# One weight load moved ahead of an activation tile, a filler product left out, two small loads moved back

## The chip, the cores and the metric

The kernel runs on one core of a Trainium2 chip. The core has a matrix engine (TensorE, PE in the profile), three engines for element work (VectorE or DVE, ScalarE or ACT, GpSimd or POOL), a queue engine that here only issues transfers (SyncE, SP) and 16 DMA engines. The metric is the device time of one execution in microseconds, as the median of several runs.

## The reference

The input x has 2048 tokens of 512 values. It is normalised over its 512 values (mean and variance, eps 1e-5). Two things are computed from the result xn and combined:

```python
Lam_bar = exp(dt * Lam);  B_bar = ((Lam_bar - 1) / Lam)[:, None] * Bmat
h = Lam_bar * h + (xn @ B_bar.T)[t]              # 2048 steps, 512 complex states
s = 2 * (h @ Cmat.T).real + xn * Dskip
g = silu((gelu(xn @ w_gate) * (xn @ w_up)) @ w_down)   # 512 -> 1376 -> 512
out = x + s * g
```

Inputs and output are bf16.

## The kernel before, in words

**Tiling.** The tokens are cut into four slabs of 512, each slab into four tiles of 128 tokens (m = 0 to 3). Slab 0 is the start of the program and is treated in a way of its own. The weights w_gate (`wg`), w_up (`wu`) and w_down (`wd`) are loaded once and stay. A product needs x with the channels on the partitions, so tiles are turned: the first three tiles of slab 0 by TensorE itself (`head_t`, with an identity matrix, into PSUM, and copied by DVE or ACT into `xcT`), everything else by DMA transposes on SP's queue (`dma_t4` for a normalised slab into `xnT`, `at_t` for a tile of the gated hidden values `at` into `atT`, and one each for the B and C matrices).

**The head.** `dummies` gives TensorE seven products of constants. `center(m)` takes the mean from a tile of x: ACT sums (L342, L350), DVE subtracts (L346, L351). `head_t(m)` turns it (L316, L331). `parameters` turns the small vectors (L606, L607). `fill` is one more product of constants into a bank that is free at that time (L305). `up_rows(m, k)` is a pair of products of row block k of w_up (128 rows, columns 0 to 1023) with tile m, into two PSUM banks (L391); the four row blocks are four loads. `first_w` does the other columns and w_gate (L421), ACT evacuates (L401, L428), `first_at` multiplies the halves (L434, L436). While that runs, DVE and GpSimd prepare statistics, angles and tables of the scan. `skip` multiplies normalised tiles by the row of D (`Drow`, L372).

**Later.** `half` makes the inputs of the scan (L550), rotates, scans and rotates back on DVE (L562 to L581) into the states `hst`; `down_pair` is the product with w_down (L484), `y_tile` the product of the states with C (L500) and the output; `gate_tile` the gated products of slabs 1 to 3 (L452).

**The order of the work.** Each step is added to a plan with the names that it reads and writes. `Plan.run` emits the steps in the order of the tuple `ORDER`, which was written out by a planner beforehand; costs and due times in the calls are the planner's and have no effect here. Each engine runs its own instructions strictly in that order, and waits on semaphores where it needs another engine's or a transfer's result. All large loads, DMA transposes and stores stand in SP's queue, in this order at the start: x tiles 0, 1, 2; w_up's four row blocks; the rest of w_up; x tile 3; w_gate in two parts; w_down's last 96 rows (L686); slab 1 of x (L217); D's row, spread over the partitions (L687); the turn of slab 0 (L367); the two turns of B (L237); the turn of `at` tile 0 (L468); w_down's other 1280 rows (L685); the turns of `at` tiles 1 and 2; the turn of slab 1; the load of slab 2; and so on. Transfers report on eight semaphores that are used in turn; a transfer is issued only when the one that used its semaphore before has landed.

Of the kernel before, what the change touches and what calls it, by code (L numbers as in the profile page):

```python
# [18 lines left out]


ORDER = (
# [23 lines left out]
)  # L45


# [33 lines left out]
def kernel(  # L81
# [46 lines left out]
    def sb(name, shape, dt=BF16):  # L128
        return consts.tile(shape, dt, name=name)
# [4 lines left out]
    wu = sb("wu", [P, KT, F])  # L134
# [50 lines left out]
    def pe(n, cols, emit, reads=(), writes=(), **kw):  # L185
        return pl.add(PE, n * (cols + 6) / 2400.0, emit, reads, writes, lag=0.22, **kw)
# [17 lines left out]
    def dma_sp(end, landed, emit, writes, **kw):  # L204

        n = dma(SP, end - sp_at[0], landed - end, emit, writes=writes, after=list(sp_last), not_before=sp_at[0], svc=(1, 0.0, 0.0), **kw)
        sp_at[0] = end
        sp_last[:] = [n]

    def load_w(nm, k0, k1, c0, c1, end, landed):  # L210

        w, r = w_of[nm]
        dma_sp(end, landed, lambda: nc.sync.dma_start(out=w[:, k0:k1, c0:c1], in_=r[:, k0:k1, c0:c1]),
               [(nm, k, c) for k in range(k0, k1) for c in range(3) if c0 <= CH[c][0] < c1])
# [6 lines left out]
    def load_x(m, end, landed):  # L221
        dma_sp(end, landed, lambda: nc.sync.dma_start(out=x_tok[:, m, :], in_=x_r[:, m, :]), [("x", 0, m)])

    W2 = CH[1][1]
    load_x(0, 1.12, 2.92)
    load_x(1, 1.59, 3.35)
    load_x(2, 2.06, 3.75)
    load_w("wu", 0, 1, 0, W2, 2.53, 5.1)
    load_w("wu", 1, 2, 0, W2, 3.0, 6.3)
    load_w("wu", 2, 3, 0, W2, 3.5, 7.4)  # L230
    load_w("wu", 3, 4, 0, W2, 4.0, 7.9)
# [53 lines left out]
    def rstd(m0, m1):  # L285

        def f():
            if m0 in BN:
                G.tensor_scalar(out=ve[:, m0:m1], in0=mv[:, m0, 1:2], scalar1=EPS, scalar2=None, op0=ALU.add)
            else:  # L290
                G.tensor_scalar(out=ve[:, m0:m1], in0=ss[:, m0:m1], scalar1=1.0 / D, scalar2=EPS, op0=ALU.mult, op1=ALU.add)
            G.tensor_tensor(out=rs[:, 0, m0:m1], in0=ve[:, m0:m1], in1=mhalf[:, m0:m1], op=ALU.pow)
        return pool(0.65 + 0.2 * (m1 - m0), f, [("mv", m) if m in BN else ("ss", m) for m in range(m0, m1)] + ["mhalf"], [("rs", 0, m) for m in range(m0, m1)],
             rank=250.0 - 20 * m0)
# [7 lines left out]
    def fill(k, i):  # L302
        def f():
            for _ in range(k):
                T.matmul(ring[i][:], lhsT=warm[:, 0:P], rhs=warm, start=True, stop=True)  # L305
        pe(k, 512, f, [], [("bank", i)])

    def head_t(m):

        if m == 0:  # L310
            for i in range(2):
                tp = ring[2 + i][:].bitcast(BF16)[:, 0 : D // 2].rearrange("p (k t) -> p k t", t=P)

                def f(i=i, tp=tp):
                    for k in range(2):
                        T.transpose(tp[:, k, :], xn[0][:, (2 * i + k) * P : (2 * i + k + 1) * P], ident[:])  # L316
                pe(2, P, f, [("xc", 0, i), "ident"], [("bank", 2 + i)])
            for i in range(2):
                tp = ring[2 + i][:].bitcast(BF16)[:, 0 : D // 2].rearrange("p (k t) -> p k t", t=P)
                dst = xcT[:, 2 * i : 2 * i + 2, 0:P]  # L320
                if i == 0:
                    head.append(dve(256, lambda tp=tp, dst=dst: V.tensor_copy(out=dst, in_=tp), [("bank", 2)], [("xcT", 0, 0)], rate=2.0, rank=500.0, after=head[-1:]))
                else:
                    acts(256, lambda tp=tp, dst=dst: act(out=dst, in_=tp, func=AF.Copy), [("bank", 3)], [("xcT", 0, 1)], rank=500.0)
            return
        bank, key = ybank[(m + 1) % 2], ("y", (m + 1) % 2)
        tp = bank[:].bitcast(BF16)[:, 0:D].rearrange("p (k t) -> p k t", t=P)

        def f():
            for k in range(KT):  # L330
                T.transpose(tp[:, k, :], xn[m][:, k * P : (k + 1) * P], ident[:])  # L331
        pe(KT, P, f, [("xc", m, 0), ("xc", m, 1), "ident"], [key])
        dve(512, lambda: V.tensor_copy(out=xcT[:, :, m * P : (m + 1) * P], in_=tp), [key], [("xcT", m, 0), ("xcT", m, 1)], rate=2.0, rank=310.0 - 20 * m)
# [331 lines left out]
        rstd(m, m + 1)  # L665
    stats(M - 1)
    rstd(M - 1, M)
    fill(1, 0)
    head_t(1)
    up_rows(0, 0)  # L670
    up_rows(1, 0)
# [174 lines left out]
```

## Time and profile before

| | us |
|---|---|
| median of 3 runs | 178.81 (178.15 to 179.05) |
| the profiled execution, device time | 178.7 |
| its span in the profile | 176.9 |
| TensorE busy | 172.0 (97% of the span) |
| VectorE busy | 157.0 (89%) |
| ScalarE busy | 123.8 (70%) |
| DMA, mean over the span | 105 GB/s |

The page of the profile lists the busy time of each engine, the span in 40 slices, the chain of work that ended last, and the costliest groups of instructions. A group is named by line, engine, operation and tiles: "L391 PE MATMUL ring<-wu,W" is a product of line 391 that reads `wu` and writes a PSUM bank of `ring` (`xcT` is a view of the tile `W`, so it shows under that name). Times in the views are microseconds from the start of the span. A matrix product's length in a row includes its way through the array; what counts in a row of many is the distance of their starts. A transfer's "us to landing" runs from the start of its issue on SP's queue to the last of the 16 counts that its DMA engines add to its semaphore.

### The profile page before, as it was taken

To read this page: it belongs to the slowest core of one execution; us is meant where nothing else is said; L and a number is where in the kernel's file an instruction comes from. 1 tells how busy PE (TensorE), PEld (TensorE's weight loads), DVE (VectorE), ACT (ScalarE), POOL (GpSimd) and SP (SyncE) were. 2 spreads that over 40 slices of the span, in tenths; PEclk is the share of its full clock that TensorE was granted. 3 is DMA by queue.
4 is the path that set the end of the run, shared out by engine and by line. 5 is a ranking of instruction groups with operands and counts; after the bars stand their busy time and mean duration, and the time that the engine had idled before them with its cause. 6 is when DMAs were issued, how large, how long until landed. Compare 5 with 4: busy or idle time off the path is not lost.

```text
span 176.9 us, 2403 instructions
## 1 busy us (share of the span) xinstructions
PE 172.0 (97%) x830; PEld 82.6 (47%) x846; DVE 157.0 (89%) x252; ACT 123.8 (70%) x236; POOL 11.3 (6%) x25
## 2 busy tenths in 40 slices
PE   8999999999999999999999999999999999999992
PEld 2554554444455544444445454444444455444451
DVE  3759999999798993999979999899999999999764
ACT  6499969969999999799578855373158618582240
POOL 2660030000200000000040000000000000000000
PEclk9999999999999999999999999999999999999999
DMA  5999999997000809423000074094000007718022
GB/s 150 311 372 230 201 235 261 205 284 143 0 0 0 200 1 186 98 79 62 0 0 6 30 139 93 31 191 85 0 0 0 0 30 158 68 34 160 26 76 76
DMA packets 48467, 18.66 MB, mean 105 GB/s; under 512 B 40296, under 2 KB 47944, under 8 KB 48456
## 3 DMA queue, kind: packets, MB, share of 16 engines
q1 hardware_dynamic: 48432, 18.52, 48.7%
q8 instruction: 6, 0.10, 0.3%
q14 instruction: 5, 0.04, 0.1%
q10 hardware_dynamic: 24, 0.00, 0.0%
HBM read 6.46 MB, written 2.10 MB: 48 GB/s over the span
## 4 chain that ended last, share of the span: by engine, by line
PE 94%; DVE 2%; DMA 1%; issue 1%; DVEq 0%
PE ring L452 31%; PE ring L484 21%; PE ring L550 16%; PE ybank L500 15%; PE ring L421 5%; PE ring L391 3%; PE ybank L421 2%; DMA x_tok<-in_A_x_dram 1%; DVE yg L505 1%; DVE junk L511 1%; PE ybank L331 0%; PE ring L316 0%; DVE yg L344 0%; PE ring L305 0%; DVE xna L346 0%
## 5 line engine op out<-in xcount | busy, mean ns | idle before, releaser
L452 PEld LDWEIGHTS <-xnT 128*128 128x128 bf16 x288 | 28.2, 98 | 28.4
L484 PE MATMUL ring<-wd,atT 128*128 128x512 bf16 (+1 forms) x171 | 38.9, 379 | 0.3
L452 PE MATMUL ring<-wg,xnT 128*128 128x512 bf16 (+1 forms) x142 | 31.4, 356 | 0.1
L452 PE MATMUL ring<-wu,xnT 128*128 128x512 bf16 (+1 forms) x142 | 31.2, 356 | 0.1
L550 PE MATMUL ring<-xnT,BT 128*128 128x512 bf16 x128 | 30.1, 379 | 0.0
L581 DVE TENSOR_TENSOR_SCAN Fs<-rho,ini,W 128x512 bf16<-128x512 f32 x24 | 29.7, 1271 | 0.1
L455 ACT ACTIVATE ub<-ring 128x512 bf16<-128x512 f32 (+1 forms) x36 | 19.2, 555 | 14.1 <-PE ring L452 14.0
L500 PE MATMUL ybank<-C,hst 128*128 128x512 bf16 x115 | 27.3, 379 | 0.3
L484 PEld LDWEIGHTS <-atT 128*128 128x128 bf16 (+1 forms) x176 | 17.2, 98 | 20.8
L552 ACT ACTIVATE U<-ring 128x512 bf16<-128x512 f32 x32 | 18.2, 600 | 7.5 <-PE ring L550 7.5
L455 ACT ACTIVATE gt<-ring 128x512 bf16<-128x512 f32 (+1 forms) x36 | 19.5, 555 | 3.7 <-PE ring L452 3.5
L500 PEld LDWEIGHTS <-hst 128*128 128x128 bf16 x136 | 13.3, 98 | 14.0
L550 PEld LDWEIGHTS <-BT 128*128 128x128 bf16 x128 | 12.5, 98 | 14.7
L487 ACT ACTIVATE g<-ring 128x512 f32<-128x512 f32 x16 | 9.4, 595 | 14.2 <-PE ring L484 14.2
L562 DVE TENSOR_TENSOR Q<-U,tab 128x4096 bf16<-128x4096 bf16 x8 | 18.3, 2289 | 0.9 <-ACT tab L649 0.7
L562 DVE TENSOR_TENSOR Q<-Fs,tab 128x4096 bf16<-128x4096 bf16 x8 | 18.3, 2287 | 0.1
L505 DVE TENSOR_TENSOR yg<-ybank,g 128x512 bf16<-128x512 f32 x15 | 10.2, 686 | 5.8 <-PE ybank L500 5.7
L764 ACT ACTIVATE junk<-x_tok 128x512 bf16<-128x512 bf16 x16 | 10.0, 633 | 0.8 <-DMA x_tok<-in_A_x_dram 0.8
L496 ACT ACTIVATE ybank<-sk 128x512 f32<-128x512 bf16 x15 | 9.1, 604 | 1.7 <-DVE yg L505 1.6
L769 ACT ACTIVATE xna<-x_tok,nb,rs 128x512 bf16<-128x512 bf16 x12 | 9.5, 812 | 0.0
L581 DVE TENSOR_TENSOR_SCAN Fs<-rho,W 128x512 bf16<-128x512 f32 x8 | 9.3, 1210 | 0.1
L461 DVE TENSOR_TENSOR at<-gt,ub 128x1024 bf16<-128x1024 bf16 x12 | 8.2, 684 | 0.1
(140 smaller groups left out, 170.6 us busy)
## 6 DMA issues: line engine op xcount, KB each, us to landing
x_tok<-in_A_x_dram SPq DMA_DIRECT2D x3, 512.0 KB, 4.1
out_dram<-ot SPq DMA_DIRECT2D x11, 128.0 KB, 1.8
wd<-in_B_w_down_dram SPq DMA_DIRECT2D x1, 1280.0 KB
wu<-in_B_w_up_dram SPq DMA_DIRECT2D x4, 256.0 KB, 4.1
wg<-in_B_w_gate_dram SPq DMA_DIRECT2D x1, 864.0 KB
x_tok<-in_A_x_dram SPq DMA_DIRECT2D x4, 128.0 KB, 2.1
wg<-in_B_w_gate_dram SPq DMA_DIRECT2D x1, 512.0 KB, 6.3
out_dram<-ot SPq DMA_DIRECT2D x6, 64.0 KB, 1.6
```

The lines of the kernel that those rows point to most:

```text
L421: T.matmul(ps[:, 0 : b - a], lhsT=lhs(k), rhs=wt[:, k, a:b], start=(k == 0), stop=(k == KT - 1))
L452: T.matmul(ps[:, 0 : b - a], lhsT=xnT[:, s % 2, m, k, :], rhs=wt[:, k, a:b], start=(k == 0), stop=(k == KT - 1))
L455: acts(b - a, lambda: act(out=dst[:, a:b], in_=ps[:, 0 : b - a], func=AF.Copy if up else AF.Gelu_apprx_tanh), [("bank", r)], [key], table= ...
L484: T.matmul(ps[:], lhsT=atT[:fs, k, m * P : (m + 1) * P], rhs=wd[:fs, k, :], start=(k == 0), stop=(k == NFT - 1))
L500: T.matmul(ps, lhsT=hst[s % 2][:, j // NPT, j % NPT, m * P : (m + 1) * P], rhs=C2[:, j // NPT, j % NPT, c0:c1], start=(j == 0 and not seed ...
L505: dve(w, lambda: V.tensor_tensor(out=yg[e][:, c0:c1], in0=ps, in1=g2[gi][:, b, c0:c1], op=ALU.mult), [key, ("g2", gi, b)], [("yg", e, c0)])
L550: T.matmul(ps[:], lhsT=BT[:, ri, k, pt * P : (pt + 1) * P], rhs=xnT[:, s % 2, :, k, :], start=(k == 0), stop=(k == KT - 1))
L552: acts(512, lambda q=q, ri=ri, ps=ps: act(out=U[ui][:, ri, q, :], in_=ps[:], func=AF.Copy), [("bank", r)], [("U", ui, q, ri)])
L562: dve(4096, lambda: V.tensor_tensor(out=Qf, in0=src.unsqueeze(1).to_broadcast(WQ), in1=table, op=ALU.mult), reads, ["Q"], rate=2.0)
L581: pl.add(DVE, 1.12 if s == 0 else 1.185, lambda ri=ri, q=q, pt=pt, first=first: V.tensor_tensor_scan(out=Fs[:, ri, q, :], data0=rho[:, pt ...
L764: acts(512, lambda i=i, fn=fn, sc=sc, m=m: act(out=junk()[:], in_=x_tok[:, s * M + m, :], func=fn, scale=sc, accum_out=sx[:, s, i, m : m + ...
L769: acts(512, lambda m=m: act(out=xn[m], in_=x_tok[:, s * M + m, :], func=AF.Identity, scale=rs[:, s, m : m + 1], bias=nb[:, s, m : m + 1]), ...
```

## The change

Four things are different.

- w_up's first row block is loaded ahead of x's tile 2; the two loads change places.
- The filler product is no longer in the program, and `ORDER`, which counts the steps, is one shorter.
- On TensorE the turn of x's tile 1 follows that of tile 0 at once, ahead of the parameters' turns; the turn of tile 2 comes after three pairs of products (block 0 with tiles 0 and 1, block 1 with tile 0) instead of one, and the pairs of tile 2 are shifted accordingly. ACT copies its half of the first turn before it sums tile 2; DVE copies its half before the parameters, and takes tile 0's statistics before it copies tile 2's turn.
- In SP's queue D's row and w_down's last 96 rows no longer stand between w_gate and the turn of slab 0. After the turn of `at` tile 0 the order is now: D's row, w_down's 1280 rows, w_down's last 96 rows, the turn of `at` tile 1. The four products with D's row of slab 0 on DVE follow `at` tile 2 instead of standing between the `at` tiles, and one of the table products (L642) goes ahead of `at` tile 2.

From there on, every engine's order is the one of before.

```diff
 ORDER = (
-    21, 22, 23, 24, 25, 0, 27, 26, 20, 18, 19, 17, 1, 40, 15, 16, 13, 14, 2, 42, 3, 4, 5, 28, 29, 30, 31, 34, 60, 33, 44, 45, 41, 61, 35, 32, 63, 43,
+    21, 22, 23, 24, 25, 0, 27, 26, 20, 18, 19, 17, 1, 40, 15, 16, 13, 14, 2, 3, 4, 5, 28, 29, 30, 31, 33, 42, 44, 45, 41, 60, 34, 32, 62, 61, 63, 67,
...
     load_x(0, 1.12, 2.92)
     load_x(1, 1.59, 3.35)
-    load_x(2, 2.06, 3.75)
-    load_w("wu", 0, 1, 0, W2, 2.53, 5.1)
+    load_w("wu", 0, 1, 0, W2, 2.06, 4.7)
+    load_x(2, 2.53, 5.0)
     load_w("wu", 1, 2, 0, W2, 3.0, 6.3)
...
     stats(M - 1)
     rstd(M - 1, M)
-    fill(1, 0)
+
     head_t(1)
     up_rows(0, 0)
     up_rows(1, 0)
```

44 rows, old and new, of the table ORDER are left out of this document.

## The prediction

> **What bounds the kernel now.** I read the page's busy shares and the chain that ended last first. They say who sets the end:
>
> ```profile
> PE 172.0 (97%) x830; PEld 82.6 (47%) x846; DVE 157.0 (89%) x252; ACT 123.8 (70%) x236; POOL 11.3 (6%) x25
> PE 94%; DVE 2%; DMA 1%; issue 1%; DVEq 0%
> ```
>
> The list of waits of TensorE from 4 us on is empty: once it has x's first tile, it never stands still until the last tile's tail. So the end is TensorE's start, plus its work, plus whatever idle time a change puts in. A gain must be work taken off TensorE; a loss is any wait that it now meets. Next, TensorE in order of time over the first 11 us (start, length, count):
>
> ```profile
> 1.57 2.34 PE L299 MATMUL ring<-const-bfloat16-1.0 128*128 128x512 bf16 x5
> 4.03 0.61 PE L316 MATMUL ring<-ident,xna 128*128 128x128 bf16 x4
> 4.57 0.18 PE L606 MATMUL ybank<-ident,pv 4*128 4x4 bf16 x1
> 4.62 0.16 PE L607 MATMUL ybank<-ident,pv 8*128 8x8 bf16 x1
> 4.71 0.61 PE L305 MATMUL ring<-const-bfloat16-1.0 128*128 128x512 bf16 x1
> 5.12 0.62 PE L331 MATMUL ybank<-ident,xna 128*128 128x128 bf16 x4
> 5.54 0.62 PE L391 MATMUL ring<-wu,W 128*128 128x512 bf16 x2
> 6.00 0.39 PE L331 MATMUL ybank<-ident,xna 128*128 128x128 bf16 x4
> 6.25 4.92 PE L391 MATMUL ring<-wu,W 128*128 128x512 bf16 x22
> ```
>
> Two paces are seen. The five dummies follow each other in (2.34 - 0.63) / 4 = 0.427 us; the 22 products in (4.92 - 0.38) / 21 = 0.216 us. The first pair of products still has 0.25 us between its starts, so the fast pace comes at about 5.6 us. A 128-column turn takes 0.107 us before that and 0.056 after.
>
> Then the DMA issues of w_up's four row blocks, each from a narrow window around its issue (KB, us to landing):
>
> ```profile
> wu<-in_B_w_up_dram SPq DMA_DIRECT2D x1, 256.0 KB, 3.0
> wu<-in_B_w_up_dram SPq DMA_DIRECT2D x1, 256.0 KB, 3.6
> wu<-in_B_w_up_dram SPq DMA_DIRECT2D x1, 256.0 KB, 4.5
> wu<-in_B_w_up_dram SPq DMA_DIRECT2D x1, 256.0 KB, 5.2
> ```
>
> Their issues begin at 2.11, 2.59, about 3.07 and 3.54, so they land at 5.1, 6.2, 7.6 and 8.75 (the counts of their semaphores in the trace say 5.13, 6.17, 7.60 and 8.75).
>
> Last, SP's queue and TensorE where the later transfers go, and the DMA's load there (last two columns: share of the 16 engines, GB/s):
>
> ```profile
> 20.88 1.74 SPq L468 DMA_TRANSPOSE atT<-at  x1
> 22.66 0.63 SPq L685 DMA_DIRECT2D wd<-in_B_w_down_dram  x1
> 23.85 7.11 SPq L468 DMA_TRANSPOSE atT<-at  x2
> 31.29 2.25 SPq L367 DMA_TRANSPOSE xnT<-xna  x1
> ```
> ```profile
> 31.32 2.97 PE L484 MATMUL ring<-wd,atT 128*128 128x512 bf16 x12
> ```
> ```profile
> 24.00:24.50 0.50, 0.50 (x5) 0.35 (x4) 0.50 (x3) 0.49 (x2) 0.00 (x0) 1.00 0.53 152
> 24.50:25.00 0.50, 0.50 (x4) 0.21 (x3) 0.50 (x2) 0.38 (x1) 0.00 (x0) 1.00 1.11 170
> 25.00:25.50 0.50, 0.50 (x5) 0.20 (x3) 0.50 (x3) 0.10 (x2) 0.00 (x0) 1.00 0.70 229
> 25.50:26.00 0.50, 0.50 (x4) 0.26 (x3) 0.50 (x2) 0.50 (x1) 0.00 (x0) 1.00 1.06 315
> ```
>
> By the semaphores w_down lands at 30.18, the second and third turned tiles of `at` at 32.17 and 33.18. The down product takes tile 0, then tile 2 (in the written order), each 11 x 0.216 = 2.38 us: tile 2 is wanted at 31.32 + 2.38 = 33.70. Its cover is only 0.5 us. This is the place to watch.
>
> **The change part by part.** The profiled execution took 178.7 us with a span of 176.9, 0.1 below the median of 178.81; I count against it.
>
> *The filler (L305) goes.* The next start follows it by 5.12 - 4.71 = 0.41 us, at the slow pace. That is the most the head can give.
>
> *The order at the head.* x's first tile is loaded first as before, so its turns stay at 4.03 to 4.43. x's second tile is centred by 4.39, so its four turns follow at once (to 4.86), then the parameters' two with the same 0.14 us around them as now. The first product can start at about 5.15. w_up's first block has one issue (0.47 us) and one tile of x less ahead of it: the second tile landed at 3.25, and the block took 1.1 us after its predecessor, so about 4.4 to 4.7. No wait; but even the old 5.13 would have done.
>
> First product pair 5.15 to 5.79 (its first half at 0.427), second pair to 6.22. The next needs block 1 (6.17): just there; to 6.65. The turn of x's third tile: its load now lands at about 5.1 instead of 4.04, its sum and centring take until 6.3 (rows of 0.63, 0.19 and 0.35 us), so TensorE meets it ready; to 6.90. One more pair to 7.33. The next needs block 2, and that lands at 7.60: TensorE waits 0.3 us. It restarts at 7.63, and after two more pairs, at 8.49, it has done what it now has done at 6.25 + 10 x 0.216 = 8.41. So the head gives nothing: +0.07. The bytes ahead of blocks 1 to 3 are the same as before, which is why they don't move; block 3 is wanted at 9.36 and covered. Bounds: -0.41 (filler fully won, block 2 0.4 us earlier) and +0.3 (block 2's first increment comes 1.6 us before its last, so one slow DMA engine can move it).
>
> *Other engines at the head.* ACT's copy of the first turn goes ahead of the third tile's sum; DVE's statistics (0.68 + 0.18) go ahead of the copy of the third turn, which is then ready at 7.6 and wanted at 8.06. The parameters' copy comes 0.7 us later, GpSimd's power after it too, but DVE takes it up at 7.58 now and 7.65 then. ACT's first evacuation (9.33) slips by 0.1; TensorE wants that bank at 12.2. Cost nothing. w_up's tail now waits for block 0's semaphore (eight are reused in turn), 4.06 to about 4.6; landed 9.75, wanted 11.01: 0.7 us would still be hidden.
>
> *Early SP queue.* w_down's last rows and D's row (issues of 0.91 and 1.10 us, 224 KB) leave. Behind them only the turn of slab 0 and the two of B come sooner; slab 0's is landed at 19.57 and used at 19.77, without a wait, so nothing is gained. The skip products move behind other DVE work of the same sum; D's row has until 25.4.
>
> *Late SP queue.* Between the first turned tile (issue done 22.62) and the second now stand D's row, w_down, w_down's last rows. An issue of such a size took 0.40 us (x's tiles) in the free queue and 1.10 in the full one. Each delays all behind it: the turns of tiles 1 and 2, slab 1's, slab 2's load, C's. Data: 224 KB at 315 GB/s are 0.7 us; the two slots from 24.0 to 25.0 are half empty, but w_down's own start-up fills them and moves by D's issue. I take D's issue at 0.55 (nearest the free queue, since 22.6 follows a single turn) plus 98 KB at 315 GB/s, 0.31: all that follows lands 0.85 us later. Bounds 0.3 and 1.4. Tile 2 then lands at 34.03; TensorE, 0.07 late, wants it at 33.77: a stall of 0.3 us (bounds 0 and 0.8). w_down itself at 30.7 is wanted at 31.4, its last rows at 31.1 at 33.5. Slab 1's turn 35.6 + 0.6 against 38.5, slab 2's load delays ACT by 0.6 at 37.69, where the banks between 47 and 55 us still have 0.7 to 1.0 us. DVE's states are done at 64.27 and wanted at 64.87; both move by about 0.3. No second stall.
>
> Sum: 178.7 + 0.07 + 0.3 = **179.1 us**.
>
> The clock's pace is where a rule speaks against the change. By the rows, the dummies end at 3.9 and until 5.6 TensorE has 0.41 us of filler now, 0.43 of real products then, and the same turns; so I leave the moment of 5.6 as it is. The Trainium skill, "TensorE: Matmul & The Clock Gate", Part 1, says that the clock is released only after a busy window of some 3.4 us, which runs free of the kernel's start, and Part 4 says that turns on TensorE don't count as busy. By that, a head of nothing but turns from 4.03 to 5.15 could miss a window; no row here shows whether turns count. That case is rival D, priced there from rows.
>
> **The rivals.**
> A (forecast): blocks of w_up take the filler's gain, tile 2 stalls a little: 178.8 to 179.6. Against it: the 33.70 is only missed if the delay exceeds 0.5.
> B: the delay of the turned tiles stays under 0.5, as the half-empty slots would allow, and block 2 comes sooner: 178.7 - 0.41 to 178.7 + 0.07, say 178.5.
> C, slower: D's and the last rows' issues take 1.10 and 0.91 us as they did in the early queue. Then tile 2 comes 1.4 us or more later, at 34.6 and after, and the stall is 0.8 to 1.3: 179.6 to 180.1, say 179.9. It decides from a delay of about 1.4 us. For it: the second turn's issue took 4.65 us (23.85 to 28.5), so the queue was full there.
> D, slower: the fast pace comes late. If it needs as long from 4.03 as it took from the first dummy at 0.76 (4.8 us), it comes at 8.85, and 3.3 us at half pace cost 1.6: 180.4.
> E, faster: the denser start brings the fast pace forward to 4.03; 1.55 us at half pace are 0.78, and with the filler 1.2: 177.5.
> F: nothing changes, because the swap buys only what block 0 had anyway; it is inside B.
>
> **How the numbers follow.** Faster or slower by 0.5% (0.9 us) is about what a measurement here can tell from no change. Chances: A 0.48, B 0.22, C 0.17, D 0.07, E 0.06. Faster is E: 0.06. Slower is C above 179.7, D and a tail of A: 0.13 + 0.07 + 0.04 = 0.24. The same: 0.70. The range leaves out E, D and a sliver of both B and C: 178.3 to 180.1.
>
> **What would show it.** No L305; TensorE's first product at 5.15; one wait for a w_up block at about 7.4; a DVE queue unchanged in sum; SP's second `atT` issue at 24.4 or later; a TensorE wait at 33.8 for `atT`. Wrong if the pace changes at another time than 5.6, if block 2 lands well off 7.6, or if tile 2 lands before 33.7.

## The result and the profile after

The changed kernel takes 179.90 us as the median of 6 runs (179.63 to 180.14), the kernel before 178.93 (178.15 to 179.18, 6 runs). The ratio is 1.0066, 95% interval 1.0046 to 1.0086: slower by two thirds of a per cent, beyond the half per cent that can be told from no change. The forecast was 179.1 and no change; 179.9 lies in the range given, but near its upper end and among the cases of the slower sign.

The profiled execution took 180.14 us with a span of 178.4, against 178.7 and 176.9 before. It is the slowest of its six, so the 1.44 us between the two profiles are more than the 0.97 between the medians. Busy times and the chain of the page after (first line: busy us, share of the span, instructions; then the chain's shares by engine and by line):

```profile
PE 172.7 (97%) x845; PEld 82.0 (46%) x845; DVE 156.9 (88%) x252; ACT 123.5 (69%) x236; POOL 12.5 (7%) x25
PE 78%; DMA 10%; DVE 9%; POOL 1%; SPq 1%; issue 0%; DVEq 0%
PE ring L452 31%; PE ring L484 20%; PE ybank L500 15%; PE ring L550 12%; DMA Drow<-in_A_Dskip_dram 3%; DMA x_tok<-in_A_x_dram 3%; DMA atT<-at 3%; DMA wu<-in_B_w_up_dram 2%; DVE Q L642 2%; DVE st L280 2%; DVE sk L372 1%; DVE yg L505 1%; DVE at L434 1%; DVE tab L642 1%; POOL rho L614 1%; DVE junk L511 1%
```

TensorE's busy time has not moved by more than 0.7 us, but its share of the chain fell from 94% to 78%: the chain now leaves TensorE and runs through transfers, and D's row (`Drow`) is one of its links. The list of TensorE's waits, empty before from 4 us on, has four rows between 4 and 45 us (us in total, times, longest); from 45 us to the end it is empty before and after:

```profile
PE ring L391 <- DMA wu<-in_B_w_up_dram: 0.8, 2, 0.6
PE ring L484 <- DMA atT<-at: 0.5, 1, 0.5
PE ring L484 <- DMA wd<-in_B_w_down_dram: 0.2, 1, 0.2
PE ring L316 <- DVE xna L346: 0.2, 1, 0.2
```

The last row is the very first turn, which begins at 4.07 instead of 4.03. The other three are the three places where the time went. (A row counts idle time from the end of the product before. That end includes some 0.16 us of its way through the array, 0.38 - 0.216, so TensorE loses about 0.16 us more at each such wait than the row says.) The head first; TensorE in order of time (start, length, what; in brackets the idle time before it that a release ended):

```profile
4.07 0.40 PE L316 MATMUL ring<-ident,xna 128*128 128x128 bf16 x4 [0.16 <-DVE xna L346]
4.49 0.40 PE L331 MATMUL ybank<-ident,xna 128*128 128x128 bf16 x4
5.21 1.02 PE L391 MATMUL ring<-wu,W 128*128 128x512 bf16 x4 [0.19 <-DMA wu<-in_B_w_up_dram]
6.85 0.59 PE L391 MATMUL ring<-wu,W 128*128 128x512 bf16 x2 [0.61 <-DMA wu<-in_B_w_up_dram]
7.28 0.38 PE L331 MATMUL ybank<-ident,xna 128*128 128x128 bf16 x4
7.50 4.05 PE L391 MATMUL ring<-wu,W 128*128 128x512 bf16 x18
11.39 1.36 PE L421 MATMUL ybank<-wu,W 128*128 128x352 bf16 x8
```

Block 0 landed at 5.17, and the first product waits 0.19 us for it. The four products of block 0 are over at 6.2, and the next pair stands until 6.85, because block 1 landed at 6.81 (6.17 before). The pace was fast from 3.99 on here and from 5.58 before, which, with the filler gone, won a part of that back. L421 begins at 11.39 where it was 11.01 before: the head lost 0.38 us.

Then SP's queue and TensorE around the down product, after:

```profile
20.94 2.28 SPq L468 DMA_TRANSPOSE atT<-at  x1
23.27 0.58 SPq L687 DMA_DIRECT2D Drow<-in_A_Dskip_dram  x1
23.89 0.43 SPq L685 DMA_DIRECT2D wd<-in_B_w_down_dram  x1
24.37 0.66 SPq L686 DMA_DIRECT2D wd<-in_B_w_down_dram  x1
25.12 7.71 SPq L468 DMA_TRANSPOSE atT<-at  x2
```
```profile
32.10 2.54 PE L484 MATMUL ring<-wd,atT 128*128 128x512 bf16 x11 [0.24 <-DMA wd<-in_B_w_down_dram]
35.11 4.93 PE L484 MATMUL ring<-wd,atT 128*128 128x512 bf16 x22 [0.47 <-DMA atT<-at]
```

Before, all three tiles of the down product ran without a break from 31.32. Now it starts at 32.10, 0.40 more than the head's 0.38, and stands again before tile 2, which starts at 35.11 instead of 33.70. So the profile's 1.44 us are 0.38 at the head, 0.40 at w_down, 0.63 at tile 2 and 0.03 in all the rest. By the counts of their semaphores w_down landed at 32.06 (30.18 before) and tile 2 at 35.07 (33.18): 1.9 us later each.

What took so long is seen in the stretches of the DMA's rate (us; busy time and instructions of each engine; the last three columns are TensorE's clock, the share of the 16 DMA engines, GB/s), after:

```profile
24.00:24.50 0.50, 0.50 (x6) 0.30 (x4) 0.49 (x1) 0.50 (x2) 0.50 (x1) 1.00 1.12 248
24.50:25.00 0.50, 0.50 (x5) 0.29 (x3) 0.00 (x0) 0.37 (x2) 0.50 (x1) 1.00 0.30 88
25.00:25.50 0.50, 0.50 (x4) 0.26 (x3) 0.07 (x1) 0.46 (x1) 0.39 (x1) 1.00 0.37 57
25.50:26.00 0.50, 0.50 (x4) 0.23 (x3) 0.50 (x2) 0.14 (x1) 0.00 (x0) 1.00 0.64 139
26.00:26.50 0.50, 0.50 (x4) 0.20 (x2) 0.45 (x2) 0.45 (x1) 0.00 (x0) 1.00 0.72 123
26.50:27.00 0.50, 0.50 (x4) 0.24 (x3) 0.00 (x0) 0.28 (x1) 0.00 (x0) 1.00 0.52 125
27.00:27.50 0.50, 0.50 (x4) 0.25 (x3) 0.00 (x0) 0.32 (x1) 0.00 (x0) 1.00 0.83 197
```

Before, the slots from 25.5 to 27.5 ran at 270 to 332 GB/s, while w_down was in flight; two of them:

```profile
26.00:26.50 0.50, 0.50 (x4) 0.23 (x3) 0.50 (x1) 0.23 (x2) 0.00 (x0) 1.00 0.95 270
26.50:27.00 0.50, 0.50 (x4) 0.20 (x2) 0.50 (x2) 0.50 (x2) 0.00 (x0) 1.00 1.05 332
```

Now, from 24.5 to 27.0, only 57 to 139 GB/s move, while D's row and w_down are both in flight. D's 16 counts come from 25.40 to 28.07, a spread of 2.7 us. VectorE stands for it, and ScalarE behind VectorE (waits of all engines, after):

```profile
DVE sk L372 <- DMA Drow<-in_A_Dskip_dram: 1.6, 1, 1.6
ACT xna L769 <- DVE sk L372: 1.3, 1, 1.3
```

### The profile page after: what moved, and what is told of

Same layout as the page of the kernel before. It is cut to its first block, busy times and chain, and to the rows that moved or that the text cites. A ratio compares the mean times of both kernels' runs of the same rounds, so it can differ in the third digit from the quotient of the medians.

```text
span 178.4 us, 2418 instructions
## 1 busy us (share of the span) xinstructions
PE 172.7 (97%) x845; PEld 82.0 (46%) x845; DVE 156.9 (88%) x252; ACT 123.5 (69%) x236; POOL 12.5 (7%) x25
## 3 DMA queue, kind: packets, MB, share of 16 engines
HBM read 6.46 MB, written 2.10 MB: 48 GB/s over the span
## 4 chain that ended last, share of the span: by engine, by line
PE 78%; DMA 10%; DVE 9%; POOL 1%; SPq 1%; issue 0%; DVEq 0%
PE ring L452 31%; PE ring L484 20%; PE ybank L500 15%; PE ring L550 12%; DMA Drow<-in_A_Dskip_dram 3%; DMA x_tok<-in_A_x_dram 3%; DMA atT<-at 3%; DMA wu<-in_B_w_up_dram 2%; DVE Q L642 2%; DVE st L280 2%; DVE sk L372 1%; DVE yg L505 1%; DVE at L434 1%; DVE tab L642 1%; POOL rho L614 1%; DVE junk L511 1%
## 5 line engine op out<-in xcount | busy, mean ns | idle before, releaser
L484 PE MATMUL ring<-wd,atT 128*128 128x512 bf16 (+1 forms) x176 | 39.5, 379 | 0.7 <-DMA atT<-at 0.5
L552 ACT ACTIVATE U<-ring 128x512 bf16<-128x512 f32 x32 | 18.1, 598 | 7.0 <-PE ring L550 7.0
```

Source lines behind the costliest of these rows:

```text
L484: T.matmul(ps[:], lhsT=atT[:fs, k, m * P : (m + 1) * P], rhs=wd[:fs, k, :], start=(k == 0), stop=(k == NFT - 1))
L552: acts(512, lambda q=q, ri=ri, ps=ps: act(out=U[ui][:, ri, q, :], in_=ps[:], func=AF.Copy), [("bank", r)], [("U", ui, q, ri)])
```

## The experiments

They ran on three chips, each with the kernel before beside it, whose median was 178.77, 178.84 or 178.66 us; each time is a median of 7 to 12 runs. In `ORDER` as changed, 115 is the step of D's row and 114 that of w_down's last rows.

**e1_head_only: the head's part alone.** D's row, w_down's last rows and the skip products stand where they stood before; the rest is the changed kernel.

```diff
-    106, 108, 95, 97, 101, 103, 107, 109, 112, 211, 212, 215, 216, 122, 98, 99, 209, 210, 213, 214, 104, 105, 124, 217, 218, 110, 111, 136, 137, 139,
+    106, 108, 95, 97, 101, 103, 107, 109, 114, 112, 211, 212, 215, 216, 122, 98, 99, 209, 210, 213, 214, 217, 115, 136, 137, 139, 141, 143, 145, 147,
...
```

> The changed kernel with D's row and w_down's last rows loaded early again, and the products with D's row back between the at tiles: the head of the change alone. Theory L (the late loads make the loss: they delay the turned tiles of at, and TensorE stands until tile 2 lands at 35.1 us): that wait is gone, tile 2 lands near 33.2 and is wanted near 34; the time is that of before plus whatever the head costs, 178.9 to 179.3. Theory H (the head makes the loss: with x's third tile behind it, w_up's blocks land late, 0.4 us in the profiled execution, and all follows): 179.5 to 179.9, little below the changed kernel.

Measured: 179.04 us against 178.77, ratio 1.0020 (1.0006 to 1.0034). The head gives nothing and costs about 0.27 us. The profiled execution, at 178.7 the fastest of its twelve, shows only the wait (TensorE in order of time):

```profile
4.91 1.06 PE L391 MATMUL ring<-wu,W 128*128 128x512 bf16 x4
6.49 0.59 PE L391 MATMUL ring<-wu,W 128*128 128x512 bf16 x2 [0.52 <-DMA wu<-in_B_w_up_dram]
11.02 1.36 PE L421 MATMUL ybank<-wu,W 128*128 128x352 bf16 x8
```

Block 1 came at 6.45, and L421 began at 11.02, as before. How the other profiles with this order of loads stand is told with e7.

**e2_late_only: the other half alone.** The head of before, with its filler and its loads; D's row and the last rows late, the skip products moved.

```diff
-    load_w("wu", 0, 1, 0, W2, 2.06, 4.7)
-    load_x(2, 2.53, 5.0)
+    load_x(2, 2.06, 3.75)
+    load_w("wu", 0, 1, 0, W2, 2.53, 5.1)
...
+    fill(1, 0)
```

> The kernel of before with D's row and w_down's last rows moved late and the products with D's row moved as in the change; the head with the filler and the old loads stays. Theory L: the turned tile 2 lands at the same absolute time as in the changed kernel, about 35.1 us, whatever the head did; TensorE, 0.4 us ahead, stands there 1.3 us instead of 0.9, and the whole loss of 1.0 us is there: 179.8 to 180.0. Theory H: about half of it, 179.3 to 179.5, since head and late part add.

Measured: 179.61 us, ratio 1.0045 (1.0024 to 1.0066). With e1's 1.0020 this gives 1.0065, the whole change's 1.0066: two losses that add, the later one the larger. TensorE at the down product:

```profile
31.22 2.54 PE L484 MATMUL ring<-wd,atT 128*128 128x512 bf16 x11
34.24 4.93 PE L484 MATMUL ring<-wd,atT 128*128 128x512 bf16 x22 [0.49 <-ACT U L552]
```

Tile 2 was wanted at 31.22 + 2.38 = 33.60 and began at 34.24, 0.04 after it had landed (34.20); the releaser named there, a row of ScalarE (L552), ended at the same moment but is not the one that matters: in e8 TensorE starts the same product at 35.37, 0.1 us before that row of ScalarE ends. The stall is 0.64, as in the whole change (35.11 - 34.48 = 0.63). Theory L had said that tile 2 lands at 35.1 whatever the head did, and a stall of 1.3; it landed 0.9 us sooner, because the queue ran ahead in this profile: the first turned tile landed at 24.19 instead of 25.09, and D's row was issued at 22.05 instead of 23.27. The counts of D's row are spread as in the whole change, from 24.44 to 27.36.

**e3_d_early and e4_rows_early: which of the two loads.** The whole change, once with D's row (115) and once with w_down's last rows (114) back in the early queue.

```diff
-    106, 108, 95, 97, 101, 103, 107, 109, 112, 211, 212, 215, 216, 122, 98, 99, 209, 210, 213, 214, 104, 105, 124, 217, 218, 110, 111, 136, 137, 139,
-    141, 143, 145, 147, 138, 140, 142, 144, 146, 148, 11, 155, 159, 174, 156, 160, 12, 157, 161, 176, 178, 151, 115, 129, 219, 158, 180, 135, 222,
+    106, 108, 95, 97, 101, 103, 107, 109, 112, 211, 212, 215, 216, 122, 98, 99, 209, 210, 213, 214, 104, 105, 124, 217, 218, 110, 111, 115, 136, 137,
+    139, 141, 143, 145, 147, 138, 140, 142, 144, 146, 148, 11, 155, 159, 174, 156, 160, 12, 157, 161, 176, 178, 151, 129, 219, 158, 180, 135, 222,
```

> The changed kernel with D's row alone loaded early again (w_down's last rows stay late). Theory S (the spread of D's row over 128 partitions is slow by itself, some 2 us for 128 KB, as its packets of 24.5 to 27 us were): w_down lands 1.3 to 1.6 us sooner than in the changed kernel, tile 2 near 33.8, no stall there or one under 0.2: 179.0 to 179.3. Theory Y (the delay goes by bytes and issues): 98 of 229 KB are still late, so 0.8 of the 1.9 us stays, tile 2 at 34.0: 179.1 to 179.4.

```diff
-    106, 108, 95, 97, 101, 103, 107, 109, 112, 211, 212, 215, 216, 122, 98, 99, 209, 210, 213, 214, 104, 105, 124, 217, 218, 110, 111, 136, 137, 139,
+    106, 108, 95, 97, 101, 103, 107, 109, 114, 112, 211, 212, 215, 216, 122, 98, 99, 209, 210, 213, 214, 104, 105, 124, 217, 218, 110, 111, 136, 137,
...
```

> The changed kernel with w_down's last rows alone loaded early again (D's row stays late). Theory S: D's row costs most of the delay of 1.9 us, 1.5 us or more; tile 2 near 34.7, TensorE stands 0.4 to 0.7 us there: 179.5 to 179.8. Theory Y: 131 of 229 KB, 1.1 us, tile 2 at 34.3, a wait of 0.2: 179.2 to 179.4.

Measured: e3 178.95 us, ratio 1.0020 (0.9991 to 1.0049); e4 179.96, ratio 1.0078 (1.0053 to 1.0103), a little over what theory S said. With D's row early no more than the head's loss is left, and the down product runs through (first fence, e3); with D's row late all of it is there, and the rate falls as in the whole change (second, e4; third, its TensorE, with the releaser named as in e2; tile 2 landed at 35.00):

```profile
31.66 7.30 PE L484 MATMUL ring<-wd,atT 128*128 128x512 bf16 x33
```
```profile
24.50:25.00 0.50, 0.50 (x6) 0.32 (x4) 0.00 (x0) 0.50 (x2) 0.50 (x1) 1.00 0.69 92
25.00:25.50 0.50, 0.50 (x4) 0.26 (x3) 0.07 (x1) 0.37 (x2) 0.40 (x1) 1.00 0.92 57
25.50:26.00 0.50, 0.50 (x4) 0.20 (x3) 0.50 (x2) 0.13 (x1) 0.00 (x0) 1.00 0.65 47
```
```profile
35.05 4.93 PE L484 MATMUL ring<-wd,atT 128*128 128x512 bf16 x22 [0.41 <-ACT U L552]
```

w_down's last rows cost nothing that can be measured in either place. The later loss is D's row alone.

**e5_distinct_rows: the same transfer from 128 different rows.** D's row is one row of 1 KB, read 128 times, once for each partition. Here the same 128 KB come from 128 rows of x; the skip term is not the reference's.

```diff
-    dma(SP, 0.7, 3.0, lambda: nc.sync.dma_start(out=Drow[:], in_=A_Dskip.partition_broadcast(P)), writes=["Drow"], after=sp_last, svc=(2, 0.5, 1.0))
+    dma(SP, 0.7, 3.0, lambda: nc.sync.dma_start(out=Drow[:], in_=B_x[0][0:P, :]), writes=["Drow"], after=sp_last, svc=(2, 0.5, 1.0))
```

> The changed kernel with one edit: the tile that holds D's row on all partitions is filled, at the same place of the queue and with the same 128 packets of 1 KB, from 128 different rows of another input instead of 128 times from D's one row (so the skip term is not that of the reference). Theory S1 (reading one and the same 1 KB 128 times is what is slow): the transfer takes about 0.5 us of the DMA engines instead of 2.5, its counts all come within 0.5 us, w_down lands near 30.8 instead of 32.1, tile 2 near 33.9, and the time falls to 179.0 to 179.3. Theory S2 (any load that starts there, after the transposes, starts slowly): nothing changes, 179.8 to 180.0.

Measured: 179.15 us, ratio 1.0020 (1.0008 to 1.0032), again what the head alone costs. The rate of the DMA, then TensorE:

```profile
24.50:25.00 0.50, 0.50 (x6) 0.34 (x4) 0.00 (x0) 0.50 (x2) 0.50 (x1) 1.00 1.18 176
25.00:25.50 0.50, 0.50 (x4) 0.25 (x3) 0.09 (x2) 0.37 (x2) 0.37 (x1) 1.00 0.73 217
25.50:26.00 0.50, 0.50 (x4) 0.20 (x2) 0.50 (x2) 0.12 (x1) 0.00 (x0) 1.00 0.95 203
26.00:26.50 0.50, 0.50 (x4) 0.23 (x3) 0.50 (x3) 0.48 (x1) 0.00 (x0) 1.00 1.00 322
```
```profile
31.86 7.30 PE L484 MATMUL ring<-wd,atT 128*128 128x512 bf16 x33
```

The counts come from 24.93 to 25.19, 0.26 us apart instead of 2.7; w_down lands at 30.42 and tile 2 at 33.64, and TensorE stands nowhere in the down product. Same bytes, same packets, same place in the queue: what the late loss needs is that they are read from one row.

**e6_no_filler: before without its filler, nothing else.**

```diff
-    fill(1, 0)
+
```

> The kernel of before without the filler product, all else as it was. Theory W (in the head TensorE meets w_up's blocks, so what the filler leaves is given to a wait): 178.5 to 178.8, a gain of 0.0 to 0.25, more of it in executions where the fast pace comes late. Theory F (the filler is pure loss): its 0.41 us at the slow pace are won, 178.3 to 178.4. Theory K (the filler keeps the clock): slower, 179.5 and more.

Measured: 178.64 us, ratio 0.9993 (0.9982 to 1.0005). TensorE:

```profile
4.72 0.60 PE L331 MATMUL ybank<-ident,xna 128*128 128x128 bf16 x4
5.25 0.95 PE L391 MATMUL ring<-wu,W 128*128 128x512 bf16 x2
6.26 4.91 PE L391 MATMUL ring<-wu,W 128*128 128x512 bf16 x22
11.01 1.36 PE L421 MATMUL ybank<-wu,W 128*128 128x352 bf16 x8
```

The turn that follows the filler starts 0.40 us sooner (4.72, 5.12 before), and the first two products 0.29 us; no wait for a load follows. But the granted clock rose at 5.99 in this profile and at 5.58 in that of before. So the two products and the turn behind them are 0.40 and 0.39 us apart where they were 0.24 and 0.22, and the 22 products begin at 6.26 instead of 6.25. In this pair of profiles the filler's time went to the slow pace, and the waits of theory W were not seen; its size fits. By the times the filler alone is worth 0.2 us by the medians (178.84 and 178.64), and by the interval anything from 0.3 gained to 0.1 lost. That rules out theories F and K; whether leaving it out gains anything is open.

**e7_old_loads: the head of e1 with x's tile 2 loaded ahead of w_up's block 0 again.** No filler, TensorE's new order of turns, the old order of loads.

```diff
-    21, 22, 23, 24, 25, 0, 27, 26, 20, 18, 19, 17, 1, 40, 15, 16, 13, 14, 2, 3, 4, 5, 28, 29, 30, 31, 33, 42, 44, 45, 41, 60, 34, 32, 62, 61, 63, 67,
+    21, 22, 23, 24, 25, 0, 27, 26, 20, 18, 19, 17, 1, 40, 15, 16, 13, 14, 3, 2, 4, 5, 28, 29, 30, 31, 33, 42, 44, 45, 41, 60, 34, 32, 62, 61, 63, 67,
```

> The head-only kernel (no filler, the new order of the turns and products, D's row and the last rows early) with the two loads back in the old order: x's third tile ahead of w_up's first block. Theory P (the swap brings w_up's second block later, 6.4 to 6.8 in the changed head against 5.9 to 6.2 in the old one, and that is the head's loss): 178.5 to 178.8, 0.3 us below the head-only kernel. Theory O (the new order of products meets block 2 earlier than it lands and loses its time there, whatever the loads): 178.9 to 179.1, the same as the head-only kernel.

Measured: 178.68 us, ratio 1.0011 (0.9984 to 1.0039). The median lies 0.16 us under that of the kernel before on its chip and the ratio 0.1% over one: two of the twelve executions took 180.75 and 180.98. The interval is too wide to part e7 from e1 or from before. On the same chip e6, the old head without its filler, has 178.64, and e5, with the new order of loads, 179.15 (that its late loads cost nothing, e9 shows below), so the medians speak for theory P.

The landings speak for its first half. In six profiles with the new order of loads (after, e1, e3, e4, e5, e8) block 1 landed at 6.81, 6.45, 6.43, 6.59, 6.97 and 7.17; in five with the old one (before, e2, e6, e7, e9) at 6.17, 5.87, 6.20, 6.42 and 5.84. No value of the one lies among the other, though 6.42 and 6.43 all but touch; the means are 0.64 us apart.

That this is what the head loses is not shown. e7's own profile, beside e1's, has no gain (TensorE):

```profile
5.36 1.69 PE L391 MATMUL ring<-wu,W 128*128 128x512 bf16 x6 [0.32 <-DVE W L333]
11.07 1.36 PE L421 MATMUL ybank<-wu,W 128*128 128x352 bf16 x8
```

L421 begins at 11.07, in e1 at 11.02. TensorE waits here too: for block 0, which landed at 5.32 (the copy L333 that is named ends at 5.37, after the product has started), and, within the six products, for block 1, where the fifth starts at 6.46 instead of 6.22. Nor do the other profiles separate the loads from TensorE's new order. The pace moves L421 as well, so only those with a like pace compare. Fast by 4.0 us, the new order of loads has 11.39 and 11.02 against 10.90 (e2); fast between 5.5 and 6.0, it has 11.56 and 11.75 against 11.01 twice (before, e6). Fast at 4.5 to 4.8, e7 has 11.07 and e9, with the same order of loads but the old order of products, 10.57. So the swap brings block 1 later, and the loss of the changed head goes with it by the medians; how much of the loss belongs to TensorE's new order stays open. Why block 1 comes later, with the same bytes ahead of it, no run shows.

**e8_x_one_row and e9_late_distinct: another row, and the late half without a repeated one.** e8 is the whole change with one row of x, read 128 times, in D's place; e9 is e2 with 128 different rows of x. Neither has the reference's skip term.

```diff
-    dma(SP, 0.7, 3.0, lambda: nc.sync.dma_start(out=Drow[:], in_=A_Dskip.partition_broadcast(P)), writes=["Drow"], after=sp_last, svc=(2, 0.5, 1.0))
+    dma(SP, 0.7, 3.0, lambda: nc.sync.dma_start(out=Drow[:], in_=B_x[0][0, :].partition_broadcast(P)), writes=["Drow"], after=sp_last, svc=(2, 0.5, 1.0))
```

> The whole change, but D's tile is filled from one row of x, read 128 times, where the run with 128 different rows of x had read each once; same place in the queue, same 128 packets of 1 KB, same array of the memory as that run. The skip term is not the reference's, the amount of work is. If it is the repetition of one address that is slow (S1), the counts spread over about 2.7 us as with D's row, w_down lands at about 32 and tile 2 of the turned gated values at about 35, and the time is that of the whole change, 179.7 to 180.1. If it is D's own place in memory (its small array, S3), the counts spread over 0.3 us as with the different rows, tile 2 lands at about 33.6, and the time is 179.0 to 179.3.

```diff
-    dma(SP, 0.7, 3.0, lambda: nc.sync.dma_start(out=Drow[:], in_=A_Dskip.partition_broadcast(P)), writes=["Drow"], after=sp_last, svc=(2, 0.5, 1.0))
+    dma(SP, 0.7, 3.0, lambda: nc.sync.dma_start(out=Drow[:], in_=B_x[0][0:P, :]), writes=["Drow"], after=sp_last, svc=(2, 0.5, 1.0))
```

> The head of before with its filler and its old order of loads; D's tile and w_down's last rows late, as in the run of the late part alone, but D's tile filled from 128 different rows of x. The skip term is not the reference's. If the slow repeated read is the whole of the late loss (S1), nothing is left of the 0.8 us that the late part cost: 178.7 to 179.0, ratio 1.000 to 1.001, and tile 2 lands by 33.4. If two more transfers in that place cost something by themselves (issue and bytes, the sum of the prediction: 0.3 us), 179.1 and a landing of 33.7 or later.

Measured: e8 179.87 us, ratio 1.0068 (1.0043 to 1.0093); e9 178.54, ratio 0.9991 (0.9972 to 1.0010). In e8 the counts spread from 25.68 to 28.58 and the rate falls (first fence), and tile 2, landed at 35.32, is waited for (second); e9's down product runs through (third):

```profile
24.50:25.00 0.50, 0.50 (x5) 0.31 (x4) 0.18 (x1) 0.50 (x2) 0.50 (x1) 1.00 0.24 80
25.00:25.50 0.50, 0.50 (x5) 0.29 (x3) 0.00 (x0) 0.37 (x2) 0.50 (x1) 1.00 0.23 59
25.50:26.00 0.50, 0.50 (x4) 0.20 (x2) 0.38 (x2) 0.32 (x1) 0.09 (x1) 1.00 0.56 111
```
```profile
35.37 4.93 PE L484 MATMUL ring<-wd,atT 128*128 128x512 bf16 x22 [0.52 <-DMA atT<-at]
```
```profile
30.89 7.30 PE L484 MATMUL ring<-wd,atT 128*128 128x512 bf16 x33
```

So it is not D's array nor its place in memory: one row of x read 128 times there does it too, and two late loads of the same size without a repeated row cost nothing. e2 and e9 differ in the source of 128 KB alone, and by 1.0045 against 0.9991.

## Why the prediction was right and wrong

**TensorE sets the end, and the loss is waits of TensorE: right.** The three places make up 1.41 of the profile's 1.44 us, and no wait follows after 45 us. "No second stall" held for that later time only: TensorE stood at w_down as well as at tile 2.

**The filler and the head: nothing gained, right; its place wrong.** e6 puts the filler alone at 0.2 us by the medians and at most 0.3, so the 0.41 were more than its leaving could give. The term of +0.07 came out at about +0.27 (e1), inside its bounds. The forecast had TensorE wait for block 2, and block 1 "just there" at 6.17, because the bytes ahead of it don't change. Block 1 came 0.3 to 1.0 us later in all six profiles with that order, and in five of them TensorE waits there (0.2 to 0.7 us); in e3, whose pace turned fast only at 6.77, the products before it were slow enough. For block 2 TensorE waited in e4 alone (0.24 us), and in e2 with the old head (0.32). Block 0 gained less than was said, too: it landed at 4.67 to 5.17, not at 4.4 to 4.7.

**The fast pace at 5.6: wrong, and not what made the loss.** By the trace's record of the granted clock it comes at 5.58 in the profile before and at 3.99 in that after; in the nine experiments anywhere from 3.69 (e2, head of before) to 6.77 (e3, head of after). Rival E said that an early pace would make the kernel faster. It was early in the profile after, and the kernel waited for block 1 all the same. Rival D's 8.85 was seen in no profile. The Trainium skill, "TensorE: Matmul & The Clock Gate", Part 1, says that the window of some 3.4 us is free-running and that the moment of release varies from run to run; the spread of 3.1 us over these profiles agrees with such a window, and is wider than the 0.5 us to either side that the same part names.

**The early queue and the other engines at the head: right.** w_up's tail was issued at 5.19 rather than 4.6, landed at 9.11 and was wanted at 11.39.

**The late queue: here the prediction failed, in one term.** The sum for tile 2's delay was 0.55 + 0.31. The 0.55 were the issue of D's row, which took 0.58. The 0.31 were "98 KB at 315 GB/s", and 98 KB are w_down's last rows, which cost nothing that could be measured (e3, e4). D's own 128 KB were given no time beside the issue: w_down was to move by that issue and by nothing else. That is the step that failed. At the forecast's own rate of 315 GB/s they would have come to an estimated 0.42 us; read from one row they left the DMA at 57 to 139 GB/s from 24.5 to 27.0.

How much that is can be counted from the landing of the first turned tile of `at`, so that a queue that runs early or late as a whole drops out. Tile 2 landed 8.44 us after it in the profile before (7.46 to 8.65 in e1, e6 and e7, which also have neither load there), 8.96 and 9.09 with different rows (e5, e9), and 9.98, 10.01, 10.03 and 10.14 with one row (after, e2, e4, e8). So the repeated read is worth about 1.0 us of tile 2's landing, where the forecast had nothing, and the two transfers in themselves, against the profile before, 0.5 to 0.65. For w_down the same count gives 5.44, then 5.74 and 5.85, then 6.94 to 7.09. The first turned tile itself landed 0.35 later after than before (25.09, 24.74). Together that is the delay of 1.9 us where 0.85 was forecast; the bound of 1.4 is passed, and the stall of 0.3 becomes 0.40 at w_down, where none was forecast, and 0.63 at tile 2. "D's row has until 25.4" was missed by 2.7 us. Whether VectorE's and ScalarE's waits for it cost anything by themselves was not tried; TensorE waits for neither in the profile after.

With different rows the forecast was too dear: e9 has no stall at all, and w_down, issued 0.73 us later in e5 than before, landed 0.24 later there. That most of such a delay is taken up is what rival B had said; that it is the half-empty slots from 24 to 25 us which do it is not shown.

**Rival C had the time and not the cause.** 179.6 to 180.1 is where the time fell, and "a delay of about 1.4 us" is where it decides; but C's price were issues of 1.10 and 0.91 us, and they took 0.58 and 0.66. Its chance of 0.17 was too small for a reason that the forecast itself had at hand: a transfer moved into the one stretch whose cover was 0.5 us had no row of its own in the trace before. There D's row landed at 16.06 us, behind a microsecond in which the rate fell to 88 and 81 GB/s; but it falls to 104 and 103 between 14.5 and 15.5 in the profile after as well, without D's row, so its price could not be read there. Nor are its counts spread in that early place: they come within 0.06 to 0.09 us in before, e1, e6 and e7 and within 0.60 in e3. What is slow is thus this read in the late place, ahead of w_down, and not shown for every place. The bounds of the delay, 0.3 and 1.4 us, came from issues and from a rate of other rows, and did not hold the 1.9.

## What to carry to other kernels

A transfer is priced by its bytes only if its source is like that of the row the rate is taken from: here one row spread over all partitions took far longer than as many different rows in the same place. Keep such a broadcast load where nothing waits behind it, as the kernel before did, and look for what is queued behind a moved load and how much cover that has. Give every moved transfer a term of its own in the sum, its bytes as well as its issue. And a profile is one execution: where the pace of TensorE differs between two of them, as with e6, a shift of some tenths of a microsecond can be the pace and not the edit.

## What the runs showed of the hardware that was not expected

- One row of 1 KB read 128 times, in front of a load of 1280 KB: the 16 counts spread over 2.7 to 2.9 us (after, e2, e4, e8), against 0.26 and 0.37 us for 128 different rows in the same place (e5, e9). In the slots of half a microsecond from 25.0 to 27.0, 28 to 68 packets of 1 KB started (after), against 99 to 183 (e5). The median packet of a slot took 46 to 51 ns in the profile after and 46 in e5, but 211 and 263 ns in e4 from 25.0 to 26.0, so whether the time is in the packets or between them differs, and what holds them back no run shows. It holds for D's array and for x. In the early place of the queue, with no large load behind it, the same row's counts came within 0.06 to 0.60 us (before, e1, e3, e6, e7).
- Two loads changed places, with the same bytes ahead of the load that follows them, and that load landed 0.64 us later in the mean of six profiles against five.
- The time at which TensorE's fast pace comes varied from 3.69 to 6.77 us over eleven profiles, and did not go with the head that the kernel had.
